# Attention heads with running sums in one bank: two key blocks give their values at once, and the scores share five banks

## The chip, the cores and the metric

The kernel runs on one core of a Trainium2 chip. Its engines are TensorE (PE, with its weight loads listed as PEld), VectorE (DVE), ScalarE (ACT), GpSimd (POOL) and SyncE (SP), whose queue issues all the DMAs. Each engine works through its own list of instructions in order and waits where a semaphore says so. Matmul results land in eight banks of PSUM, each 512 float32 columns wide on 128 partitions.

The metric is the time of one execution in microseconds of the device. Before the change it is 2222.45 us, the median of three runs (2220.9 to 2225.58).

## The reference

Four layers act on x of 2048 positions by 640 features, all in float32. Layers 1 and 3 are attention, layers 2 and 4 a Fourier mixing, and each is added to its input after a layer norm:

```
x = x + _A_ref(_layernorm(x), A_wqkv, A_wo)        # attention
x = x + _B_ref(_layernorm(x), seq_re, seq_im, hid_re, hid_im)
x = x + _A_ref(_layernorm(x), A_wqkv, A_wo)
x = x + _B_ref(_layernorm(x), seq_re, seq_im, hid_re, hid_im)
```

Attention has 32 heads of 20 features and a sliding window: position i sees positions j with 0 <= i - j < 256.

```
scores = einsum("bhqd,bhkd->bhqk", q, k) * (Dh ** -0.5)
mask = (idx[:, None] - idx[None, :] >= 0) & (idx[:, None] - idx[None, :] < W)
p = _softmax(where(mask, scores, -1e9))
o = einsum("bhqk,bhkd->bhqd", p, v);  out = o.reshape(B, S, D) @ wo
```

The Fourier layer multiplies by cosine and sine matrices over features and over positions and keeps the real part. The change leaves it alone.

## The kernel before, in words

Every layer takes its turn on the same core. The change lies in the part of an attention layer that the code calls heads (`heads`, line 597), which runs twice, once in each attention layer.

**Blocks and steps.** Positions are cut into 16 blocks of 128, heads into 8 groups of four ("quads"). With the window of 256, a key block meets at most three query blocks: its own and the next two. One step of the loop in line 770 is one key block of one quad, so there are 16 x 8 = 128 steps in an attention layer, after ten steps of lead. In each step the loop runs two halves, z = 0 and z = 1, for two of the four heads each. A half issues, in this order:

- T (`t_pair`, line 646; matmuls of line 650): the scores of key block t, with keys on the partitions, for its query blocks, up to 384 columns. Two heads run side by side in the upper and the lower 64 rows of the array, each into a bank of its own.
- S (`s_head`, line 617; matmuls of line 622): the scores of query block s = t + 10, this time with queries on the partitions, for two heads into two more banks. DVE adds the mask and takes the row maximum (line 627; the profile shows it as CUSTOM_DVE and DVE_READ_ACCUMULATOR2, which writes tile `mc`). The maximum is what T, ten steps later, gets subtracted through an extra row of its operands.
- the exponential (`t_exp`, line 654; ACT, line 660): both banks of T in one instruction, into tile `pt`; then POOL zeroes what lies outside the window (`t_mask`, lines 666 and 670).
- every fourth step, in z = 1: `m_rows` (line 632): PE transposes the maxima of four query blocks (line 635), ACT copies them negated (line 638) and SP sends them to the row of `qp`.
- in z = 1: PV (`pv`, line 676; matmuls of line 685): the products of exponentials and values for query block t - 1. For each of three key blocks and four heads it is one matmul of 128 columns with 32 columns of weights; the four heads stand side by side in the array. The twelve accumulate in one bank, and ACT copies its 128 columns to `ou` (line 692).
- in z = 0: `fill` (line 745): a few pairs of matmuls of other work. For most of the heads stage this is the projection of later quads (`project`, `pieces`, matmuls of line 253 in pairs of 64-row halves, 512 columns each), then the first three fifths of the output product (`partials`, 320 columns each).

Projection results leave their banks (6 and 7) by an ACT copy (line 540) and are cut into a high and a low part: POOL casts the high part (line 543), DVE subtracts (line 207). Jobs like these wait in lanes, one lane per engine, and `tick` (line 172) starts one of each lane at the end of every half.

**Banks.** T, S, PV and `m_rows` share six banks, 0 to 5. Which bank a use gets is settled when the program is written: `borrow` and `borrow_pair` (lines 136 and 144) keep for each bank the time at which it would be free by the constants of lines 40 to 42, and take the earliest. A T pair gets two neighbouring banks. The waits then follow from the tiles: an instruction that touches a bank waits for the last one that used it.

**Order.** All of this is written in one order by `heads`; no scheduler moves it. On each engine the instructions stand as the code issues them.

Of the kernel before, what the change touches and what calls it, by code (L numbers as in the profile page):

```python
# [40 lines left out]
AT_T, AT_S, AT_PV = (0.0, 1.28), (0.18, 1.46), 1.7  # L41
HELD_T, HELD_S, HELD_PV = 1.4, (0.96, 1.54), 1.3
# [5 lines left out]
    "m": (6, 7), "f": (6, 7, 4, 5), "w": (6, 7, 2, 3),  # L48
# [15 lines left out]
class Net:  # L64
# [71 lines left out]
    def borrow(self, at, *held):  # L136

        free = self.ring6
        got = sorted(free, key=lambda b: (free[b], b))[:len(held)]
        for b, d in zip(got, held):  # L140
            free[b] = max(at, free[b]) + d
        return got

    def borrow_pair(self, at, held):

        free = self.ring6
# [25 lines left out]
    def tick(self):  # L172
        self.slot += 1
        for k in sorted(k for k in self.posted if k <= self.slot):
            for f in self.posted.pop(k):
                f()
        for lane in self.lanes.values():
            if lane and lane[0][0] <= self.slot:
                lane.popleft()[2]()
# [18 lines left out]
    def sub_job(self, lane, key, lo, src, hi, done=None):  # L198

        eng = {"dve": self.nc.vector, "pool": self.nc.gpsimd}[lane]  # L200
        n = 2 if lane == "pool" else 1
        w = src.shape[-1] // n
        for i in range(n):
            c = slice(i * w, (i + 1) * w)

            def sub(c=c, last=i == n - 1):
                eng.tensor_tensor(out=lo[..., c], in0=src[..., c], in1=hi[..., c].bitcast(F32), op=OP.subtract)  # L207
                if last and done:
                    done()
            self.job(lane, key, sub)  # L210
# [141 lines left out]
    def attention(self, xsrc, xdst):  # L352
        self.take_small(F32)
        for name in ("kp", "qp"):
            for i in (1, 0):
                if (name, i) != ("kp", 0):
                    self.take_qk(name, i)
        self.after, self.wide, self.lead = False, False, True
        self.late_o, self.late_t, self.part_t, self.packable = [], 0, 0, set()
        self.before_heads(xsrc)  # L360
        self.heads(xsrc, xdst, self.fourier_hook)
        self.after_heads()
# [160 lines left out]
    def pieces(self, c, sbs, role):  # L523
# [13 lines left out]
        def copied(p, sb):  # L537
            st = self.work.tile([P, 2, 512], F32R, name="c", tag="c", bufs=3)
            r = self.raw()[:, :512]
            self.nc.scalar.activation(r, p, AF.Copy)  # L540

            def cast():
# [4 lines left out]
            def store():  # L547
                self.store_qk(c, sb, st)
                self.packable.add((c, sb))
            self.job("pool", ("qk", c, sb), cast)  # L550
# [46 lines left out]
    def heads(self, xsrc, xdst, hook):  # L597
# [56 lines left out]
        def t_exp(quad, kb, z, banks):  # L654
            n = min(NB - kb, 3)
            b0, b1 = banks
            if z == 0:
                i = 0 if (quad, kb) == (NQ - 1, NB - 1) else kb % 4
                pt[quad, kb] = self.pt[i].rearrange("p (h s) -> p h s", h=4)
            nc.scalar.activation(pt[quad, kb][:, 2 * z:2 * z + 2, :n * P], self.banks[:, b0:b1 + 1, :n * P],  # L660
                                 AF.Exp, scale=SCALE)
# [14 lines left out]
        def pv(quad, qb, bank):  # L676
# [4 lines left out]
            for kb in range(max(qb - 2, 0), qb + 1):  # L681
                t = pt[quad, kb]
                vq = self.vq[(4 * quad + kb // 4) % 3]
                for h in range(4):
                    nc.tensor.matmul(  # L685
                        self.banks[32 * h:32 * h + 32, bank, :P],
                        vq[:, 96 * (kb % 4) + 21 * h:96 * (kb % 4) + 21 * h + 32],
                        t[:, h, (qb - kb) * P:(qb - kb + 1) * P],
                        start=kb == max(qb - 2, 0), stop=kb == qb,
                        tile_position=(0, 32 * h), skip_group_check=True)  # L690
            pt.pop((quad, qb - 2), None)
            nc.scalar.activation(ous[quad, bk][:, at:at + P], self.banks[:, bank, :P], AF.Copy)
            if qb % 4 == 3:
                finish(quad, bk)
# [50 lines left out]
        def fill(n):  # L745

            k, size = 0, 1
            while k < size:
# [6 lines left out]
                if k == 1:  # L755
                    left = self.left + 1
                    size = -(-left // max(1, round(left / n)))
# [11 lines left out]
        self.ring6 = dict.fromkeys((0, 1, 2, 3), -99.0)  # L769
        for step in range(-LEAD, steps + 1):  # L770
            now[0] = step
            clock = step * STEP
            if step == -1:
                self.ring6.update({4: -99.0, 5: -99.0})
            if step + LEAD == steps + 1:
                for b in ROLES["w"]:
                    self.ring6.pop(b, None)
            self.wide, self.lead, self.tiled = step + LEAD > steps, step < -2, step < steps - 1
# [12 lines left out]
            if v >= 0 and v % 4 == 3:  # L791
                load_v(v // 4 + 2)
# [7 lines left out]
            rows = ((s - 1) // 16, ((s - 1) % 16) // 4) if 4 <= s < steps + 4 and s % 4 == 0 else None  # L800
            for z in range(2):
                if 0 <= t < steps:
                    banks = self.borrow_pair(clock + AT_T[z], HELD_T)
                    t_pair(t // 16, t % 16, z, banks)
                if 0 <= s < steps:
                    for e, b in enumerate(self.borrow(clock + AT_S[z], *HELD_S)):
                        s_head(s // 16, s % 16, 2 * z + e, b)
                if z and (rows or 0 <= v < steps):
                    last, = self.borrow(clock + AT_PV, HELD_PV)
                m = m_rows(*rows, last) if z and rows else iter(())  # L810
# [7 lines left out]
                if z:  # L818
                    if 0 <= v < steps:
                        pv(v // 16, v % 16, last)  # L820
                    for _ in m:
                        pass
                if z == 0 or t < -1 or t >= steps:
                    fill(nf)
# [121 lines left out]
    def partials(self, xsrc):  # L946
# [5 lines left out]
        for t in range(NB):  # L952
# [8 lines left out]
            ps = [self.bank("w" if self.wide else "m", 320) for _ in range(2)]  # L961
# [848 lines left out]
```

## Time and profile before

| | us |
|---|---|
| median of three runs | 2222.45 |
| the profiled execution, its own time | 2220.75 |
| its span, first instruction to last | 2219.0 |
| PE busy in the span | 2131.4 |
| DVE busy | 1669.5 |
| ACT busy | 1126.6 |
| POOL busy | 910.6 |
| first and last PV matmul of the program | 163.4 and 1638.6 |

The profile was taken on one execution; its times are microseconds from the start of the span unless marked ns. A busy PE includes the time that a result takes through the array, so a full row of it is no sign of a full array. The two heads stages lie at 163 to 538 us and at 1265 to 1639 us. PEclk is the granted clock of TensorE as a share of full speed. A releaser, named behind an arrow, is what ended a wait; a timeline row with a count covers several instructions of one kind that follow each other.

### The profile page before, as it was taken

The page shows a single profiled execution, that of the slowest core. Times are in us where ns is not written, and L with a number is a line of the kernel's source. Part 1 is how long each engine was busy: PE and PEld are TensorE (multiplying, and loading weights), DVE is VectorE, ACT ScalarE, POOL GpSimd, SP SyncE. Part 2 cuts the span into 40 slices and gives each one's busy share as a digit, 9 for nine tenths or more (in the row PEclk, how much of TensorE's full clock was granted, in tenths as well). Part 3 has the DMA queues.
Part 4 walks back from the last instruction along what each step waited for, and adds up shares of the span by engine and source line. Part 5 has one row for each costly group of instructions (what it writes and reads, how often), then busy time and mean ns, then how long its engine had stood idle before and what let it go on. Part 6 is the DMA issues. An engine that isn't in the chain of part 4 may idle for free.

```text
span 2219.0 us, 49084 instructions
## 1 busy us (share of the span) xinstructions
PE 2131.4 (96%) x17908; PEld 1786.0 (80%) x17908; DVE 1669.5 (75%) x4031; ACT 1126.6 (51%) x2101; POOL 910.6 (41%) x1456
## 2 busy tenths in 40 slices
PE   7999999998989999999999999998989999999999
PEld 7987777677868888889999777776777688888899
DVE  7368888785897968776651788887858978687776
ACT  3127776656554545552431377676655545455332
POOL 3016565666613223232330266566665132341334
PEclk9999999899999999999999999999999999999999
DMA  5545565775435354665646456657855354546653
GB/s 196 176 160 190 182 190 192 225 208 175 142 124 176 128 185 133 215 202 193 205 147 191 151 189 183 199 184 225 211 160 157 115 182 137 174 143 216 223 169 120
DMA packets 220177, 392.11 MB, mean 177 GB/s; under 512 B 39200, under 2 KB 85792, under 8 KB 219936
## 3 DMA queue, kind: packets, MB, share of 16 engines
q1 hardware_dynamic: 219936, 388.98, 55.6%
q8 instruction: 141, 2.31, 0.5%
q14 instruction: 100, 0.82, 0.1%
HBM read 273.94 MB, written 113.77 MB: 175 GB/s over the span
## 4 chain that ended last, share of the span: by engine, by line
PE 70%; DVE 13%; issue 6%; DMA 4%; ACT 3%; POOL 3%; SPq 0%; ACTq 0%; DVEq 0%; POOLq 0%
PE banks L1360 28%; PE banks L235 13%; PE banks L253 9%; PE banks L685 5%; PE banks L650 5%; DVE banks L627 5%; PE banks L1648 4%; PE banks L622 4%; DMA qp<-qk_d 1%; DVE c L207 1%; POOL big L228 1%; DVE mc L627 1%; DMA qk_d<-c 1%; DVE qp L228 1%; PE banks L337 1%
## 5 line engine op out<-in xcount | busy, mean ns | idle before, releaser
L627 DVE CUSTOM_DVE_ANT_0 banks<-banks,mask 128x384 f32<-128x384 f32 (+2 forms) x1024 | 526.8, 556 | 98.5 <-PE banks L622 80.5
L660 ACT ACTIVATE pt<-banks 128x768 f32<-128x768 f32 (+2 forms) x512 | 394.3, 772 | 179.0 <-PE banks L650 74.0
L666 POOL TENSOR_SCALAR_AFFINE_SELECT pt<-pt 128x256 f32<-128x256 f32 x512 | 215.8, 422 | 282.0 <-ACT pt L660 243.2
L253 PE MATMUL banks<-big,wc 64*128 64x512 f32 x1920 | 271.2, 394 | 0.4 <-DVE pt L438 0.4
L650 PE MATMUL banks<-qp,kp 61*128 61x384 f32 (+2 forms) x1024 | 211.8, 383 | 32.5 <-DVE mc L627 28.5
L685 PE MATMUL banks<-pt,vq 128*32 128x128 f32 x5760 | 213.4, 280 | 1.5 <-ACT pt L660 1.5
L622 PE MATMUL banks<-kp,qp 60*128 60x384 f32 (+2 forms) x1024 | 204.9, 352 | 6.6 <-DVE mc L627 4.1
L670 POOL TENSOR_SCALAR_AFFINE_SELECT pt<-pt 128x256 f32<-128x256 f32 x448 | 207.2, 462 | 0.0
L253 PEld LDWEIGHTS banks<-big,wc 64*128 64x128 f32 x1920 | 186.5, 185 | 22.9 <-ACT x L540 1.7
L650 PEld LDWEIGHTS banks<-qp,kp 61*128 61x128 f32 x1024 | 108.6, 186 | 100.4 <-DVE mc L627 76.5
L685 PEld LDWEIGHTS banks<-pt,vq 128*32 128x32 f32 x5760 | 143.4, 110 | 49.5 <-issue 36.4
L222 ACT ACTIVATE c<-pt 128x512 fp32r<-128x512 f32 x150 | 93.6, 626 | 160.3 <-POOL pt L1280 52.9
L222 ACT ACTIVATE qp<-pt 128x512 fp32r<-128x512 f32 (+1 forms) x195 | 119.9, 624 | 105.3 <-DVE pt L1294 54.0
L228 DVE TENSOR_TENSOR c<-pt,c 128x512 fp32r<-128x512 f32 x150 | 123.0, 822 | 52.0 <-ACT c L222 49.9
L228 DVE TENSOR_TENSOR qp<-pt,qp 128x512 fp32r<-128x512 f32 (+1 forms) x191 | 151.2, 799 | 11.7 <-ACT qp L222 9.0
L1360 PE MATMUL banks<-qp,big 128*128 128x512 f32 x630 | 152.4, 394 | 2.9 <-POOL qp L228 1.7
L1293 POOL TENSOR_TENSOR pt<-pt,pt 128x512 f32<-128x512 f32 x34 | 50.7, 1490 | 237.1 <-DMA pt<-c 145.9
L622 PEld LDWEIGHTS banks<-kp,qp 60*128 60x128 f32 x1024 | 119.9, 188 | 32.1 <-DVE mc L627 19.5
L627 DVE DVE_READ_ACCUMULATOR2_ANT mc<- 128x1 f32 x1024 | 144.3, 141 | 0.0
L1360 PEld LDWEIGHTS banks<-qp,big 128*128 128x128 f32 x630 | 119.0, 190 | 28.8 <-POOL qp L228 2.3
L1360 PE MATMUL banks<-qp,xc 128*128 128x512 f32 x480 | 117.2, 390 | 0.7 <-DVE xc L228 0.7
L543 POOL CAST c<-x 128x512 fp32r<-128x512 f32 x64 | 40.3, 633 | 181.3 <-ACT x L540 180.3
(246 smaller groups left out, 4475.0 us busy)
## 6 DMA issues: line engine op xcount, KB each, us to landing
pt<-c SPq DMA_DIRECT2D x188, 512.0 KB
qk_d<-c SPq DMA_DIRECT2D x80, 512.0 KB
kp<-qk_d SPq DMA_DIRECT2D x384, 80.0 KB
qp<-qk_d SPq DMA_DIRECT2D x384, 80.0 KB
kp<-u_d SPq DMA_DIRECT2D x32, 640.0 KB
o_d<-ou SPq DMA_DIRECT2D x64, 256.0 KB
x_d<-x SPq DMA_DIRECT2D x48, 320.0 KB
v_d<-pt SPq DMA_DIRECT2D x16, 768.0 KB
```

What stands on the lines that cost most here:

```text
L222: nc.scalar.activation(hi, src, AF.Copy, scale=-1.0 if neg else 1.0)
L228: (eng or nc.vector).tensor_tensor(out=lo, in0=src, in1=hi.bitcast(F32), op=OP.subtract)
L235: self.nc.tensor.matmul(p, x, y, start=n == 0, stop=n == last)
L253: self.nc.tensor.matmul(ps[a], x[r], y[r], start=half + i == 0, stop=half == 1 and i == n - 1, skip_group_check=True)
L622: nc.tensor.matmul(p, qp[quad % 2][b:b + 60, z, qb * P:(qb + 1) * P], kp[quad % 2][b:b + 60, z, k0 * P:(qb + 1) * P], start=True, stop=True)
L627: nc.vector.tensor_tensor_reduce(out=p, in0=p, in1=self.mask[:, 384 - n * P:], scale=1.0, scalar=NEG, op0=OP.add, op1=OP.max, accum_out=mc ...
L650: nc.tensor.matmul(self.banks[:, banks[e], :n * P], kp[quad % 2][b:b + 61, z, kb * P:(kb + 1) * P], qp[quad % 2][b:b + 61, z, kb * P:(kb + ...
L660: nc.scalar.activation(pt[quad, kb][:, 2 * z:2 * z + 2, :n * P], self.banks[:, b0:b1 + 1, :n * P], AF.Exp, scale=SCALE)
L666: nc.gpsimd.affine_select(out=t[:, :, 0:P], in_=t[:, :, 0:P], pattern=[[0, 2], [1, P]], compare_op=OP.is_ge, fill=0.0, base=0, channel_mul ...
L670: nc.gpsimd.affine_select(out=t[:, :, 256:384], in_=t[:, :, 256:384], pattern=[[0, 2], [-1, P]], compare_op=OP.is_gt, fill=0.0, base=0, ch ...
L685: nc.tensor.matmul(self.banks[32 * h:32 * h + 32, bank, :P], vq[:, 96 * (kb % 4) + 21 * h:96 * (kb % 4) + 21 * h + 32], t[:, h, (qb - kb) ...
L1360: nc.tensor.matmul(self.banks[:, bk, :], p, b[q], start=start and m == 0, stop=stop and last and m == 2, skip_group_check=True)
```

## The change

Six things change, all in the heads stage:

1. PV runs every second step, for two key blocks at once, and is turned around: each key block gives its values to all its query blocks (up to 384 columns in one matmul of each head, or two where the columns wrap). The sums run on in bank 5, which holds four query blocks of 128 columns. No matmul starts a sum; instead ACT writes zeros over a pair of query blocks (`clear`) after it has copied them out (`sums`, 256 columns instead of two copies of 128). `v` is t - 2.
2. T, S and `m_rows` share five banks, 0 to 4. A T pair takes the two banks that are free first, whether they are neighbours or not, and its exponential reads them as one slice with a step. New constants say when and how long a bank is held, and S and `m_rows` of a half may not take the banks of its T pair.
3. `fill` gets exact sizes: nine pairs in z = 0 and none in z = 1 of a step with PV, five and four in the step without; while projections last, about three quarters of the rate and none, then a half and a half.
4. The low part of the projection results is subtracted by POOL in two pieces of 256 columns instead of by DVE in one of 512, in a chain that starts only while fewer than three `c` buffers are in use.
5. In the lead, `tick` starts two jobs of each lane.
6. The banks 2 and 3 are no longer used for the last outputs within the heads stage.

```diff
-AT_T, AT_S, AT_PV = (0.0, 1.28), (0.18, 1.46), 1.7
-HELD_T, HELD_S, HELD_PV = 1.4, (0.96, 1.54), 1.3
+AT_T, AT_S, AT_M = ((0.0, 0.95), (0.4, 1.45)), 0.18, 1.5
+HELD_T, HELD_S, HELD_M = 1.4, (0.96, 1.54), 1.2
+SUMS = 5
+SIZES = ((9, 0), (5, 4))
...
     def borrow_pair(self, at, held):
-        free = self.ring6
-        b = min((b for b in free if b + 1 in free),
-                key=lambda b: (max(free[b], free[b + 1], at), -min(free[b], free[b + 1]), b))
-        free[b] = free[b + 1] = max(free[b], free[b + 1], at) + held
-        return b, b + 1
+        free = self.ring5
+        got = sorted(sorted(free, key=lambda b: (free[b], b))[:2])
+        for b in got:
+            free[b] = max([at] + [free[b] for b in got]) + held
+        return got
...
-            st = self.work.tile([P, 2, 512], F32R, name="c", tag="c", bufs=3)
             r = self.raw()[:, :512]
+            key = "qk", c, sb
             self.nc.scalar.activation(r, p, AF.Copy)
...
+            def lead():
+                if self.c_live == 3:
+                    self.post(1, lambda: self.job("pool", key, lead))
+                    return
+                self.c_live += 1
+                st = self.work.tile([P, 2, 512], F32R, name="c", tag="c", bufs=3)
                 self.nc.gpsimd.tensor_copy(st[:, 0, :], r)
-                self.sub_job("dve", ("qk", c, sb), st[:, 1, :], r, st[:, 0, :],
-                             lambda: self.post(2, store))
+                self.sub_job("pool", key, st[:, 1, :], r, st[:, 0, :], lambda: self.post(2, lambda: store(st)))
...
-            nc.scalar.activation(pt[quad, kb][:, 2 * z:2 * z + 2, :n * P], self.banks[:, b0:b1 + 1, :n * P],
+            nc.scalar.activation(pt[quad, kb][:, 2 * z:2 * z + 2, :n * P], self.banks[:, b0:b1 + 1:b1 - b0, :n * P],
                                  AF.Exp, scale=SCALE)
...
+        def pv(quad, kb):
+            n, a = min(NB - kb, 3), kb % 4
+            vq = self.vq[(4 * quad + kb // 4) % 3]
+            t = pt.pop((quad, kb))
+            d0 = 0
+            while d0 < n:
+                d1 = min(n, d0 + 4 - (a + d0) % 4)
+                at = (a + d0) % 4 * P
+                for h in range(4):
+                    nc.tensor.matmul(
+                        self.banks[32 * h:32 * h + 32, SUMS, at:at + (d1 - d0) * P],
+                        vq[:, 96 * (kb % 4) + 21 * h:96 * (kb % 4) + 21 * h + 32],
+                        t[:, h, d0 * P:d1 * P], start=False, stop=d0 == 0,
+                        tile_position=(0, 32 * h), skip_group_check=True)
+                d0 = d1
+        def clear(c0, c1):
+            nc.scalar.activation(self.banks[:, SUMS, c0:c1], self.half.broadcast_to([P, c1 - c0]), AF.Copy, scale=0.0)
...
-            nc.scalar.activation(ous[quad, bk][:, at:at + P], self.banks[:, bank, :P], AF.Copy)
-            if qb % 4 == 3:
+            nc.scalar.activation(ous[quad, bk][:, at:at + 2 * P], self.banks[:, SUMS, at:at + 2 * P], AF.Copy)
+            clear(at, at + 2 * P)
+            if at:
                 finish(quad, bk)
...
-            s, t, v = step + LEAD, step, step - 1
+            s, t, v = step + LEAD, step, step - 2
...
-                if z == 0 or t < -1 or t >= steps:
-                    fill(nf)
+                if not 0 <= t < steps:
+                    if z == 0 or t < -1 or t >= steps:
+                        fill(nf)
+                elif not (z and visit):
+                    fill(SIZES[not visit][z] if done[0] >= total else round(nf * (0.75 if visit else 0.5)), True)
```

What it moves shows in the built programs. In the rows below, names stand as in the code (`pt`, `ou`, `banks`), the sizes are those of the output, and the brackets hold the semaphores that an instruction waits for, each named after the engine that raises it. `half` as a source marks `clear`.

ACT in steps 57 to 59 of layer 1 (quad 3), before: the copy of PV (L692) stands behind every second exponential (L660), and the copy of the maxima (L638) behind it in every fourth step.

```order
L660 ACTIVATE pt_95<-banks 128x768 [waits PE_49,Activation_49,Pool_49]
L660 ACTIVATE pt_95<-banks 128x768 [waits PE_49,Pool_49]
L692 ACTIVATE ou_98<-banks 128x128 [waits DMAHW3_49,DMAHW2_49,PE_49]
L660 ACTIVATE pt_96<-banks 128x768 [waits PE_49,Activation_49,Pool_49]
L660 ACTIVATE pt_96<-banks 128x768 [waits PE_49,Pool_49]
L692 ACTIVATE ou_98<-banks 128x128 [waits PE_49]
L638 ACTIVATE mt<-banks 16x128 [waits DMAHW1_49,DMAHW0_49,Activation_49]
```

ACT at the same place after, steps 56 to 58; the exponentials are L668, the copies L709, the zeros L702.

```order
L668 ACTIVATE pt_94<-banks 128x768 [waits DVE_49,Pool_49] x2
L709 ACTIVATE ou_99<-banks 128x256 [waits PE_49,Activation_49]
L702 ACTIVATE banks<-half 128x256 [waits Activation_49]
L668 ACTIVATE pt_95<-banks 128x768 [waits PE_49,Pool_49]
L668 ACTIVATE pt_95<-banks 128x768 [waits DVE_49,Pool_49]
L668 ACTIVATE pt_96<-banks 128x768 [waits DVE_49,Pool_49]
L668 ACTIVATE pt_96<-banks 128x768 [waits DVE_49,PE_49,Pool_49]
L709 ACTIVATE ou_98<-banks 128x256 [waits DMAHW0_49,DMAHW1_49,PE_49,Activation_49]
```

In the rows before, an exponential waits for PE, that is for its own two T matmuls, and for things long done. In the rows after, five of the six wait for DVE. Where a T pair lies in banks 0 and k, the slice with a step is treated as all the banks from 0 to k, and a maximum of S that works in a bank between them counts as a writer. The semaphore's count says which: it is the maximum of an S head of the same half, issued just ahead of the exponential. So it is in 163 of the 236 halves of layer 1 that have an S: in 132 it is the second head's, in 31 the first's; the other 73 have their pair in banks 0 and 1, or no S between.

PE around a PV with `m_rows`, steps 74 and 75 of layer 1, before. L622 is S, L635 the transposition of the maxima, L685 PV, L650 T.

```order
L622 MATMUL banks<-kp_103,qp_104 128x384 [waits DVE_49]
L622 MATMUL banks<-kp_103,qp_104 128x384 [waits Activation_49]
L635 MATMUL banks<-ident,mc 16x128
L685 MATMUL banks<-pt_97,vq_93 32x128 x4
L685 MATMUL banks<-pt_94,vq_91 32x128 x4
L685 MATMUL banks<-pt_95,vq_91 32x128 [waits Pool_49]
L685 MATMUL banks<-pt_95,vq_91 32x128
L685 MATMUL banks<-pt_95,vq_91 32x128 [waits Pool_49]
L685 MATMUL banks<-pt_95,vq_91 32x128
L650 MATMUL banks<-qp_105,kp_560 128x384 [waits DVE_49]
L650 MATMUL banks<-qp_105,kp_560 128x384
L622 MATMUL banks<-kp_103,qp_104 128x384 [waits Activation_49]
```

PE around such a PV after, steps 58 and 59; the two S matmuls of the half (L630) stand just ahead of these rows. L643 is the transposition, L694 PV, L658 T.

```order
L643 MATMUL banks<-ident,mc 16x128 [waits DVE_49]
L694 MATMUL banks<-pt_94,vq_93 32x384 [waits DMAHW4_49,Pool_49]
L694 MATMUL banks<-pt_94,vq_93 32x384
L694 MATMUL banks<-pt_94,vq_93 32x384 [waits Pool_49]
L694 MATMUL banks<-pt_94,vq_93 32x384
L694 MATMUL banks<-pt_95,vq_93 32x384 [waits Pool_49]
L694 MATMUL banks<-pt_95,vq_93 32x384
L694 MATMUL banks<-pt_95,vq_93 32x384 [waits Pool_49]
L694 MATMUL banks<-pt_95,vq_93 32x384
L658 MATMUL banks<-qp_104,kp_103 128x384 [waits Activation_49]
L658 MATMUL banks<-qp_104,kp_103 128x384
L630 MATMUL banks<-kp_560,qp_105 128x384 [waits Activation_49]
```

Twelve PV matmuls of 128 columns in each step became eight of 384 in every second one (sixteen where columns wrap). The transposition now takes the bank of an S head of its own half and waits for its maximum; S of the next half takes that bank and waits for ACT's copy of the transposed rows. The first T head has bank 0 in 234 of those 236 halves, so it waits for the exponential of the half before.

More of the change, by code (lines that the diff above doesn't have):

```diff
@@ L817, in heads @@
                     self.relieve()
[L818 to L822, printed above, removed]
[L823 to L824 removed]
+                if z and visit:
+                    for kb in (v % 16, v % 16 + 1):
+                        pv(v // 16, kb)
+                    sums(v // 16, v % 16)
+                for _ in m:
+                    pass
+                if not 0 <= t < steps:
[3 more added lines that the diff above has]
+                    fill(SIZES[not visit][z] if done[0] >= total else round(nf * (0.75 if visit else 0.5)), True)
                 self.tick()
```

70 lines of the change are left out of this document (30 added, 40 removed).

## The prediction

> **What bounds the kernel now.** I read the page first, for what the heads stage does most.
>
> ```profile
> span 2219.0 us, 49084 instructions
> ...
> L627 DVE CUSTOM_DVE_ANT_0 banks<-banks,mask 128x384 f32<-128x384 f32 (+2 forms) x1024 | 526.8, 556 | 98.5 <-PE banks L622 80.5
> L660 ACT ACTIVATE pt<-banks 128x768 f32<-128x768 f32 (+2 forms) x512 | 394.3, 772 | 179.0 <-PE banks L650 74.0
> ```
>
> The span is 1.75 us under the execution's own 2220.75, which lies 1.7 under the median; my sum goes from 2220.75. The maxima cost DVE more than the exponentials cost ACT, and neither waits much. Next the busy times by windows, of the exponentials alone, and of all engines for the middle of the stage. A step holds two exponentials, so half the count is steps.
>
> ```profile
> 163.00:438.00 275.00, 148.05 (x192) 0.97 0.62 194
> 163.00:515.00 352.00, 183.96 (x239) 0.98 0.65 196
> 515.00:538.00 23.00, 10.76 (x16) 1.00 0.32 97
> 208.00:386.00 178.00, 98.60 (x128) 1.00 0.60 189
> 208.00:386.00 178.00, 171.73 (x2442) 130.14 (x2437) 153.42 (x559) 126.47 (x232) 107.16 (x255) 1.00 0.60 189
> ```
>
> While projections last, 96 steps take 275 us, 2.86 each. The next 23.5 steps (47 exponentials in 77 us), with the output product, take 3.28 each; the last 8, without S, 2.9. In the middle PE is busy for 172 of 178 us and DVE for 153: all engines overlap, PE and DVE bind together. The timeline of one step shows how:
>
> ```profile
> 1380.03 0.45 PE L650 MATMUL banks<-qp,kp 61*128 61x384 f32 x2
> 1380.16 0.28 ACT L692 ACTIVATE ou<-banks 128x128 f32<-128x128 f32 x1 [0.33 <-PE banks L685]
> 1380.31 0.34 PE L622 MATMUL banks<-kp,qp 60*128 60x384 f32 x2
> 1380.49 0.86 PE L253 MATMUL banks<-big,wc 64*128 64x512 f32 x6
> 1380.59 0.81 ACT L660 ACTIVATE pt<-banks 128x768 f32<-128x768 f32 x1
> 1380.68 0.57 DVE L627 CUSTOM_DVE_ANT_0 banks<-banks,mask 128x384 f32<-128x384 f32 x1 [0.53 <-PE banks L622]
> 1381.16 0.14 DVE L627 DVE_READ_ACCUMULATOR2_ANT mc<- 128x1 f32 x1
> 1381.16 0.60 DVE L627 CUSTOM_DVE_ANT_0 banks<-banks,mask 128x384 f32<-128x384 f32 x1
> 1381.39 0.60 ACT L540 ACTIVATE x<-banks 128x512 f32<-128x512 f32 x1
> 1381.68 0.14 DVE L627 DVE_READ_ACCUMULATOR2_ANT mc<- 128x1 f32 x1
> 1381.83 0.86 PE L685 MATMUL banks<-pt,vq 128*32 128x128 f32 x24
> 1382.62 0.45 PE L650 MATMUL banks<-qp,kp 61*128 61x384 f32 x2
> 1382.84 0.87 DVE L207 TENSOR_TENSOR c<-x,c 128x512 fp32r<-128x512 f32 x1
> ```
>
> From T to T of the next step pass 2.59 us. The exponential starts while the two maxima of its half have yet to run: the two branches after T and S are parallel. That is what the change touches.
>
> **The change part by part.** *The exponential's wait.* After the change, five exponentials in seven wait for a maximum of their own half, and the next half's T waits for that exponential (its bank 0). So T, S, maximum, exponential and next T stand in one chain, and nothing of a later half can begin beside it on PE. Two more links of that chain, from the timeline near the end of the stage (T, exponential, T) and from one place where an exponential now follows a maximum:
>
> ```profile
> 517.90 0.81 ACT L660 ACTIVATE pt<-banks 128x768 f32<-128x768 f32 x1 [0.69 <-PE banks L650]
> ...
> 518.76 0.44 PE L650 MATMUL banks<-qp,kp 61*128 61x384 f32 x2 [0.17 <-ACT pt L660]
> ...
> 519.31 0.81 ACT L660 ACTIVATE pt<-banks 128x768 f32<-128x768 f32 x1 [0.37 <-PE banks L650]
> ```
>
> ```profile
> 361.60 0.14 DVE L627 DVE_READ_ACCUMULATOR2_ANT mc<- 128x1 f32 x1
> 361.79 0.81 ACT L660 ACTIVATE pt<-banks 128x768 f32<-128x768 f32 x1 [0.41 <-DVE mc L627]
> ```
>
> A half whose exponential waits for the second head's maximum ("S1") lasts: T to S 0.28 (1380.03 to 1380.31), S to maximum 0.37, both maxima 1.14 (1380.68 to 1381.82), to the exponential 0.05 (361.74 to 361.79), itself 0.81, to the next T 0.05 (518.71 to 518.76): 2.70 us. With the first maximum alone (0.62, to 1381.30) it is 2.18 ("S0"). Where only T is waited for ("P") it is 0.55 (518.76 to 519.31) + 0.81 + 0.05 = 1.41.
>
> *PV, the transposition, the copies.* Two rows of PE where the transposition of the maxima goes ahead of PV:
>
> ```profile
> 401.54 0.28 PE L635 MATMUL banks<-ident,mc 128*16 128x128 f32 x1
> 401.75 0.86 PE L685 MATMUL banks<-pt,vq 128*32 128x128 f32 x24
> ```
>
> Two steps had two PVs of 24 rows of 128 columns (a float32 matmul shows as two rows), 1.72 in all. After, they have one of 16 rows of 384 columns, the same columns in a third of the rows. By columns it costs the 1.72 less one of the two ends, a result's way through the array (a pair of T shows 0.45 from start to end for 384 columns, a set of PV rows some 0.27): 1.45. By rows it would be 0.57, 16 of 24 rows at 0.86. I take columns, since pairs of other widths differ with the width (three of 512 columns took 0.86, one of 384 took 0.34), and keep 0.57 as the low end. In an S1 half, PV (0.28 + 0.29 + 1.45 = 2.02) hides behind the chain's 2.70. Every second visit the transposition must wait for the first maximum (0.28 + 0.37 + 0.62 + 0.05 = 1.32), with PV behind it (0.21 + 1.45), and T behind PV: 3.0. The next half's S then waits for ACT's copy of the transposed rows, which stands behind the copy of the sums and the zeros; S starts some 0.7 late: 2.9 instead of 2.18. Copies: two of 0.28 become one of 256 columns and one clear, 0.38 each by interpolation between 0.28 (128 columns) and 0.60 (512); they lie on ACT in a gap of the chain (0.81 busy in 2.70) except there.
>
> *The sum at full clock.* In 12 steps the 24 halves, by the semaphores: z = 0 with PV to follow, 4 S1 and 2 P, 13.6; z = 1 with PV, 3 S1 and 3 with transposition, 17.1; z = 0 after it, one S0, two at 2.9, three P of 1.7 (PV's tail still in the way), 13.2; z = 1 without PV, 13.6. Together 57.5, 4.79 a step. Steps with short T and S take off 0.2, and fill's wait for a bank's second copy (every 8 steps) adds 0.15: 4.74 against 2.86.
>
> *The clock.* Windows across the two places where PE had least to do in this stage; the third figure from the right is the granted clock.
>
> ```profile
> 417.00:420.00 3.00, 2.04 (x32) 1.16 (x32) 3.00 (x9) 1.85 (x5) 3.00 (x6) 1.00 0.56 171
> 420.00:424.00 4.00, 3.71 (x36) 2.36 (x38) 2.69 (x11) 1.81 (x4) 1.74 (x5) 0.57 0.89 252
> 424.00:427.00 3.00, 2.50 (x31) 1.42 (x29) 2.28 (x8) 1.13 (x2) 1.51 (x3) 0.50 0.93 275
> ...
> 434.00:437.00 3.00, 3.00 (x32) 2.60 (x26) 1.99 (x9) 1.09 (x2) 1.21 (x4) 0.50 0.65 176
> ...
> 1519.00:1523.00 4.00, 2.66 (x37) 1.53 (x37) 3.91 (x14) 2.46 (x5) 2.91 (x7) 1.00 0.67 186
> ```
>
> PE busy for 2.04 of 3 us brought the clock to half; it came back only after a stretch with PE full (3.00 of 3). 2.66 of 4 kept it. After the change a chain half without PV has T 0.45, S 0.34 and one or two pairs of fill (0.86/3 = 0.29 each), about 1.1 to 1.3 of 2.70, under half: the clock must fall there. What a half lasts then, from the second half of those rows' stretch (PE, and DVE's next maximum):
>
> ```profile
> 430.96 0.69 PE L650 MATMUL banks<-qp,kp 61*128 61x384 f32 x2
> 431.45 0.52 PE L622 MATMUL banks<-kp,qp 60*128 60x384 f32 x2
> 432.01 0.57 DVE L627 CUSTOM_DVE_ANT_0 banks<-banks,mask 128x384 f32<-128x384 f32 x1 [1.24 <-PE banks L622]
> 433.31 1.51 PE L685 MATMUL banks<-pt,vq 128*32 128x128 f32 x24
> ```
>
> T to S 0.49, S to maximum 0.56: S1 3.10, S0 2.58, P 1.65 to 2.1. PV, twice 1.51 less a tail, about 2.7, no longer hides: 3.7 with PV, 4.85 with the transposition too. The 12 steps take 72.5, and with the same edges 6.0 each. A PV half then fills PE, and may bring the clock back if such a stretch falls right, for a stretch: I take four fifths at half clock, 4.74 + 0.8 x 1.26 = 5.75. With PV at its low end it would be 5.3.
>
> [...]
>
> *What moves off the chain.* DVE loses the subtractions (0.87 each, one in two steps), POOL gets two of 256 columns for each; the nearest row of POOL:
>
> ```profile
> L885 POOL TENSOR_TENSOR x<-x,rr x48: 724/734/1047, 405.7 to 1613.6; 128x256 f32<-128x256 f32 x48
> ```
>
> 1.47 us in two steps of POOL, which is busy 107 of 178 and would have steps twice as long: hidden, at nothing; DVE's gain is worth nothing either, since the maxima wait for S now. Without the chain it would be up to 0.4 a step, which the last rival uses. The bigger tick in the lead, the later `c` buffer and the last outputs' banks lie in spare time. Where projections end, the steps before wait for loads (the exponentials again):
>
> ```profile
> 415.00:438.00 23.00, 8.32 (x13) 0.63 0.77 232
> ```
>
> 6.5 steps at 3.54 instead of the 2.78 of the stage's middle: 5 us, which longer steps absorb, -5 a layer.
>
> *The sum.* A layer: 96 x (5.75 - 2.86) = 277; the later 23.5 steps have more fill (nine, five and four pairs), so the clock holds better: 4.6 at full and 6.0 at half clock, 4.9 taken, 23.5 x (4.9 - 3.28) = 38; the last eight, without S, 3.2 for 2.9, 3; loads -5. That is 313, twice 626: 2220.75 + 626 = 2847 us.
>
> **The rivals.** *Full clock throughout.* PV and fill in visits keep the clock up, as 1519 to 1523 did with 2.66 of 4: 96 x 1.88 = 180, 23.5 x 1.32 = 31, 3, -5: 209 a layer, 2639 us. *All at half clock*: 301 + 63 + 12 - 5 = 371, 2963.
>
> *The exponential isn't held by the maxima* (DVE's mark is reached early, because S ran ahead): then only T, exponential, T binds. Four steps have six halves of 1.41, one with PV at 2.0, one with the transposition at 3.0, and 0.5 trails behind these: 14.0, 3.5 a step. That is 61, and 7 for the later steps, 68 a layer, 2357. Against it: T, S and the exponential's wait belong to one half, and S stands behind T in PE's list.
>
> *Faster.* The waits cost nothing, because ring and order give way, and PV is paid by instruction (0.57 for 1.72 in two steps). DVE then bounds a step, freed of its subtraction: its four maxima take 2.28, the quiet step above 2.59, and between them 2.45 instead of 2.86 gives 96 x 0.41 x 2 = 79, 2142 us. It decides if an S1 half takes under 1.4 us, which two maxima of 1.14 in front of an exponential of 0.81 exclude. It would need the semaphore not to hold at all.
>
> That the change does nothing has no room: the wait and the bank 0 are in the program.
>
> **How the numbers follow.** The serial chain at mostly half clock 0.60 (2847; some 2760 with PV at its low end); the same at full clock 0.20; all half or worse, say through late loads, 0.10; 2357 0.06; faster 0.03; no change 0.01. The range leaves out the last three and most of the "worse": 2620 to 2960. What a measurement here can tell from no change is some 0.2%, 4.4 us; by the cases, faster 0.03, same 0.01, slower 0.96.
>
> **What would show it.** In the profile after: ACT idle ahead of L668 on `mc`, released by DVE, in some 160 of 236 halves a layer; PE idle ahead of L658 on `pt`, released by ACT; 5 to 6 us for two exponentials in the middle of the stage; PEclk near 0.5 to 0.6 in the heads slices; PV rows about three times longer in streaming, visits under 3 us at full clock; L643 waiting for DVE. Wrong would be the forecast if the clock stays at 1.00 (then 2639), if exponentials start before their half's maxima end (2357 or less), or if steps exceed 6.5 us, which loads or POOL's masks and subtractions on the chain would do.

## The result, and the profile after

The changed kernel takes 2877.2 us (median of 4 runs, 2866.9 to 2884.5) against 2223.2 us, a ratio of 1.294 (95% interval 1.289 to 1.299). The profiled execution took 2882.5 us, 1.7 more than its span; so its sums stand 5 us above the median.

The page, first the lines that answer to those shown of before:

```profile
span 2880.8 us, 43356 instructions
...
L635 DVE CUSTOM_DVE_ANT_0 banks<-banks,mask 128x384 f32<-128x384 f32 (+2 forms) x1024 | 528.0, 557 | 779.2 <-PE banks L630 765.3
L668 ACT ACTIVATE pt<-banks 128x768 f32<-128x768 f32 (+2 forms) x512 | 393.2, 769 | 715.8 <-DVE mc L635 577.3
```

The same instructions take the same time, 557 ns a maximum and 769 an exponential. What grew is the idle time ahead of them: 779 us before the maxima, which wait for S (98.5 before), and 716 before the exponentials (179.0), 577 of it ended by DVE's maxima. How much of the waiting before the exponentials DVE's maxima ended, in both layers, before and then after (us, times):

```profile
  DVE mc L627: 4.5, 11
```

```profile
  DVE mc L635: 577.3, 290
```

Windows of the exponentials alone: the 96 steps with projections, the next 24, the last 8, and then the same 178 us that were shown of before. The fifth row has all engines in these 178 us; in the window rows PEclk stands third from the right.

```profile
163.00:723.00 560.00, 147.92 (x193) 0.68 0.32 97
723.00:841.00 118.00, 37.30 (x48) 0.92 0.50 136
841.00:864.00 23.00, 11.13 (x16) 1.00 0.27 80
208.00:386.00 178.00, 45.79 (x61) 0.66 0.30 91
208.00:386.00 178.00, 129.26 (x807) 70.92 (x807) 69.78 (x256) 63.37 (x110) 57.85 (x134) 0.66 0.30 91
```

Two exponentials are a step: 5.80 us a step for 2.86, 4.9 for 3.28, 2.9 for 2.9. No engine is full any more: PE 129 of 178 us (172 before), DVE 70 (153), at two thirds of the clock. This is the picture of a chain. One half of it at full clock, on the timeline:

```profile
407.57 0.45 PE L658 MATMUL banks<-qp,kp 61*128 61x384 f32 x2 [0.35 <-ACT pt L668]
...
407.86 0.37 PE L630 MATMUL banks<-kp,qp 60*128 60x384 f32 x2
...
408.23 0.57 DVE L635 CUSTOM_DVE_ANT_0 banks<-banks,mask 128x384 f32<-128x384 f32 x1 [0.18 <-PE banks L630]
...
408.71 0.60 DVE L635 CUSTOM_DVE_ANT_0 banks<-banks,mask 128x384 f32<-128x384 f32 x1
409.23 0.14 DVE L635 DVE_READ_ACCUMULATOR2_ANT mc<- 128x1 f32 x1
409.47 0.81 ACT L668 ACTIVATE pt<-banks 128x768 f32<-128x768 f32 x1 [1.94 <-DVE mc L635]
...
410.33 0.69 PE L658 MATMUL banks<-qp,kp 61*128 61x384 f32 x2 [1.42 <-ACT pt L668]
```

T to S 0.29, S to maximum 0.37, the maxima 1.14 to 409.37, 0.10, the exponential 0.81, 0.05: from T to T 2.76 us, in which PE waits for 1.42. The next half, from 410.33 on, has the transposition and PV, now at half clock:

```profile
412.05 0.38 PE L643 MATMUL banks<-ident,mc 128*16 128x128 f32 x1 [0.72 <-DVE mc L635]
412.36 2.79 PE L694 MATMUL banks<-pt,vq 128*32 128x384 f32 x16
415.08 0.69 PE L658 MATMUL banks<-qp,kp 61*128 61x384 f32 x2
416.31 0.69 PE L630 MATMUL banks<-kp,qp 60*128 60x384 f32 x2 [0.54 <-ACT mt L646]
```

From T at 410.33 to T at 415.08 it takes 4.75 us: the transposition waits for the maximum, PV follows, and the next S waits for ACT's copy. The windows around it show the clock go:

```profile
406.00:410.00 4.00, 2.42 (x18) 1.55 (x18) 2.28 (x8) 1.43 (x3) 1.54 (x4) 1.00 0.43 131
410.00:413.00 3.00, 1.95 (x9) 0.79 (x13) 1.14 (x4) 0.65 (x2) 0.77 (x2) 0.56 0.00 0
413.00:416.00 3.00, 2.77 (x18) 0.68 (x10) 0.00 (x0) 1.14 (x3) 0.77 (x2) 0.50 0.03 5
```

PE was busy for 2.42 of 4 us, and the clock went to half. The trace lists every change of the clock. In this stage of this run the granted clock was either full or half (1.00 or 0.50), and its changes lay 3.41 us or whole multiples of that apart. Here are four stretches of this length, in each of which the clock was constant: after the first it rose to full, through the second it stayed there, after the third it fell to half, after the fourth it rose.

```profile
400.11:403.52 3.41, 3.17 (x36) 1.89 (x36) 1.25 (x5) 0.99 (x2) 0.79 (x3) 0.50 0.50 163
403.52:406.93 3.41, 2.15 (x24) 1.30 (x16) 1.16 (x5) 1.80 (x4) 1.51 (x4) 1.00 0.26 82
406.93:410.35 3.42, 1.65 (x16) 0.92 (x12) 2.26 (x8) 1.40 (x2) 0.77 (x3) 1.00 0.27 74
427.42:430.83 3.41, 3.41 (x36) 2.02 (x28) 0.69 (x6) 2.23 (x4) 1.47 (x3) 0.50 0.00 0
```

Over the first heads stage, 168 to 864 us, the clock fell after 37 such stretches, in which PE was busy for 19 to 60%, and stayed full through 53 with 55 to 100%. It rose after 38 with 84 to 100%, and stayed at half through 74 with 29 to 93%. Between 55 and 60% both are found, a fall and none, and from 84 to 93% both a rise and none, so PE's busy share alone doesn't tell the cases apart. The waits of PE in the heads stage of layer 1, summed (us, times, longest):

```profile
PE banks L658 <- ACT pt L668: 133.3, 139, 2.1
PE banks L643 <- DVE mc L635: 20.7, 29, 1.2
PE banks L630 <- ACT mt L646: 20.3, 29, 0.9
PE banks L256 <- ACT x L543: 17.0, 12, 2.2
```

No single wait is longer than 2.2 us, and still a third of the clock is missing in the steps with projections.

### The profile page after: what moved, and what is told of

Its sections match the earlier page's. It is cut to its first block, busy times and chain, and to the rows that moved or that the text cites. A ratio compares the mean times of both kernels' runs of the same rounds, so it can differ in the third digit from the quotient of the medians.

```text
span 2880.8 us, 43356 instructions
## 1 busy us (share of the span) xinstructions
PE 2441.5 (85%) x14964; PEld 1835.4 (64%) x14964; DVE 1636.9 (57%) x3967; ACT 1160.6 (40%) x2103; POOL 981.4 (34%) x1584
## 4 chain that ended last, share of the span: by engine, by line
PE 62%; ACT 12%; DVE 11%; issue 7%; DMA 4%; POOL 3%; SPq 1%; ACTq 0%; DVEq 0%; POOLq 0%
PE banks L1382 22%; PE banks L238 10%; PE banks L694 8%; ACT pt L668 7%; PE banks L256 7%; PE banks L658 6%; DVE banks L635 5%; PE banks L630 4%; PE banks L1670 4%; DVE mc L635 2%; ACT ou L709 1%; PE banks L643 1%; POOL big L231 1%; ACT mt L646 1%; PE banks L340 1%
## 5 line engine op out<-in xcount | busy, mean ns | idle before, releaser
L635 DVE CUSTOM_DVE_ANT_0 banks<-banks,mask 128x384 f32<-128x384 f32 (+2 forms) x1024 | 528.0, 557 | 779.2 <-PE banks L630 765.3
L668 ACT ACTIVATE pt<-banks 128x768 f32<-128x768 f32 (+2 forms) x512 | 393.2, 769 | 715.8 <-DVE mc L635 577.3
L658 PE MATMUL banks<-qp,kp 61*128 61x384 f32 (+2 forms) x1024 | 283.1, 512 | 270.8 <-ACT pt L668 267.8
L674 POOL TENSOR_SCALAR_AFFINE_SELECT pt<-pt 128x256 f32<-128x256 f32 x512 | 213.2, 416 | 875.3 <-ACT pt L668 858.5
L658 PEld LDWEIGHTS banks<-qp,kp 61*128 61x128 f32 x1024 | 137.3, 234 | 515.9 <-ACT pt L668 449.1
L256 PE MATMUL banks<-big,wc 64*128 64x512 f32 x1920 | 379.3, 489 | 34.6 <-ACT x L543 33.8
L256 PEld LDWEIGHTS banks<-big,wc 64*128 64x128 f32 x1920 | 235.7, 239 | 69.8 <-ACT x L543 50.1
L630 PE MATMUL banks<-kp,qp 60*128 60x384 f32 (+2 forms) x1024 | 241.8, 428 | 42.1 <-ACT mt L646 40.8
L694 PE MATMUL banks<-pt,vq 128*32 128x384 f32 (+2 forms) x2816 | 276.8, 545 | 0.0
L630 PEld LDWEIGHTS banks<-kp,qp 60*128 60x128 f32 x1024 | 147.4, 247 | 68.8 <-ACT mt L646 57.6
L678 POOL TENSOR_SCALAR_AFFINE_SELECT pt<-pt 128x256 f32<-128x256 f32 x448 | 186.1, 415 | 0.0
L694 PEld LDWEIGHTS banks<-pt,vq 128*32 128x32 f32 x2816 | 98.4, 142 | 105.5 <-issue 82.7
L635 DVE DVE_READ_ACCUMULATOR2_ANT mc<- 128x1 f32 x1024 | 145.3, 142 | 0.0
L709 ACT ACTIVATE ou<-banks 128x256 f32<-128x256 f32 x128 | 49.0, 383 | 135.3 <-PE banks L694 135.2
```

The lines of the kernel that those rows point to most:

```text
L256: self.nc.tensor.matmul(ps[a], x[r], y[r], start=half + i == 0, stop=half == 1 and i == n - 1, skip_group_check=True)
L630: nc.tensor.matmul(p, qp[quad % 2][b:b + 60, z, qb * P:(qb + 1) * P], kp[quad % 2][b:b + 60, z, k0 * P:(qb + 1) * P], start=True, stop=True)
L635: nc.vector.tensor_tensor_reduce(out=p, in0=p, in1=self.mask[:, 384 - n * P:], scale=1.0, scalar=NEG, op0=OP.add, op1=OP.max, accum_out=mc ...
L658: nc.tensor.matmul(self.banks[:, banks[e], :n * P], kp[quad % 2][b:b + 61, z, kb * P:(kb + 1) * P], qp[quad % 2][b:b + 61, z, kb * P:(kb + ...
L674: nc.gpsimd.affine_select(out=t[:, :, 0:P], in_=t[:, :, 0:P], pattern=[[0, 2], [1, P]], compare_op=OP.is_ge, fill=0.0, base=0, channel_mul ...
L678: nc.gpsimd.affine_select(out=t[:, :, 256:384], in_=t[:, :, 256:384], pattern=[[0, 2], [-1, P]], compare_op=OP.is_gt, fill=0.0, base=0, ch ...
```

## The experiments

**Two ways to take the maxima out of the chain.** First, neighbouring banks again:

```
-        got = sorted(sorted(free, key=lambda b: (free[b], b))[:2])
-        for b in got:
-            free[b] = max([at] + [free[b] for b in got]) + held
-        return got
+        b = min((b for b in free if b + 1 in free),
+                key=lambda b: (max(free[b], free[b + 1], at), -min(free[b], free[b + 1]), b))
+        free[b] = free[b + 1] = max(free[b], free[b + 1], at) + held
+        return b, b + 1
```

> The changed kernel, with one thing put back: a T pair takes two neighbouring banks again (of five), so that its exponential's slice holds no third bank. In the built program no exponential waits for a maximum of its own half. Theory (the wait for the maxima puts T, S, maximum and exponential in one chain, and PE's idle time in it halves the clock): the chain is T, exponential, T in about half of the halves, 3.0 to 3.7 us a step, the clock near 1.00 through the heads, 2300 to 2420 us. Rival (the turned PV, its zeros and copies, and the exact fill are what costs): 2700 us or more, with steps of 5 us.

2386.3 us, ratio to before 1.072 (1.069 to 1.074). Second, the change's own banks, but one exponential for each bank:

```
-            nc.scalar.activation(pt[quad, kb][:, 2 * z:2 * z + 2, :n * P], self.banks[:, b0:b1 + 1:b1 - b0, :n * P],
-                                 AF.Exp, scale=SCALE)
+            for e in range(2):
+                nc.scalar.activation(pt[quad, kb][:, 2 * z + e, :n * P], self.banks[:, banks[e], :n * P],
+                                     AF.Exp, scale=SCALE)
```

> The changed kernel with the exponential of a half as two instructions, one for each bank of the T pair; the banks stay as the change picks them, and T's first head still takes bank 0. No exponential waits for a maximum. Theory: as with neighbouring banks the maxima leave the chain; two exponentials of 384 columns cost about 0.49 each (from 0.60 at 512 and 0.81 at 768), but the next T waits for the first of them alone: 2280 to 2400 us, clock near 1.00. Rival (bank 0 held from half to half is the cause, not the maxima): 2600 us or more. Rival (PV and fill): 2700 or more.

2389.9 us, ratio 1.075 (1.072 to 1.077). The exponentials by windows, with neighbouring banks and then with two exponentials for each half:

```profile
208.00:386.00 178.00, 74.05 (x98) 0.97 0.48 143
```

```profile
208.00:386.00 178.00, 82.52 (x200) 0.99 0.50 149
```

49 and 50 steps in 178 us, 3.6 each, where the change does 30.5; the clock is back (0.97 and 0.99 for 0.66). Both edits take the wait for the maxima out, each in another way, and both bring some 490 us. Neither changes the wait alone: the first also takes T off bank 0 in about two thirds of the halves, worked through the code, the second frees bank 0 after the first of two exponentials. What they share is the wait, and the second still reads the two distant banks. So the slice with a step costs by what it is taken to touch, and not by reading distant banks; the exponential itself took no longer (769 ns for 772). All the rest of the change, the turned PV and bank 0 among it, makes 161 to 164 us net without the wait.

**The clock alone.** The chain stays, and PE is given matmuls that change nothing, in 79 of the 256 halves of a layer (counted from the rows of T, 2604 for 1024):

```
                     for e, b in enumerate(self.borrow(at + AT_S, *HELD_S, but=banks)):
                         s_head(s // 16, s % 16, 2 * z + e, b)
+                    if banks and banks[0] < b < banks[1] and not (z and visit):
+                        for _ in range(5):
+                            t_pair(t // 16, t % 16, z, banks)
```

> The changed kernel, and in every half whose exponential waits for the second head's maximum and which has no PV, the two T matmuls are issued five times more behind S. They write what already stands there, and 0.8 us of matmuls fit into the 1.5 us in which PE waits there, so they prolong no chain. Theory (a third of the loss is the clock, which falls because PE idles): the granted clock in the heads rises from 0.67 to over 0.9, steps go from 5.8 to about 4.9 us, 2640 to 2740 us. Rival (the low clock is no cause: what it slows is hidden in the chain, or it doesn't follow PE's idle time): 2860 us or more.

2765.0 us, ratio 1.242 (1.240 to 1.244). The 96 steps with projections, exponentials alone, then the steps after them:

```profile
160.00:654.00 494.00, 147.67 (x192) 0.92 0.36 109
654.00:782.00 128.00, 37.91 (x49) 0.87 0.48 127
```

More work on PE made the kernel 112 us faster. The clock went from 0.68 to 0.92, the steps from 5.80 to 5.15. That is less than I expected, and the later steps, with more fill of their own, got longer (5.2 for 4.9, their clock 0.87 for 0.92), so the added matmuls were not all free. At least 112 of the 654 us are the clock.

**The banks' choice alone, in the kernel before.** Six banks, the old PV; only `borrow_pair` (not printed again) and the slice of the exponential are the change's:

```
...
-            nc.scalar.activation(pt[quad, kb][:, 2 * z:2 * z + 2, :n * P], self.banks[:, b0:b1 + 1, :n * P],
+            nc.scalar.activation(pt[quad, kb][:, 2 * z:2 * z + 2, :n * P], self.banks[:, b0:b1 + 1:b1 - b0, :n * P],
```

> The kernel before with the banks of a T pair picked as the change picks them, the two that are free first, and the slice with a step; six banks, PV and all else as before. 82 exponentials of 512 then wait for the second maximum of their half, 134 for the first. Theory: such halves take 2.70 and 2.18 us instead of 1.43 where the next T waits for the exponential, which 226 T matmuls now do: some 100 us a layer if all of it shows, about half if the third pair of banks gives slack: 2300 to 2500 us. Rival (ACT has time to wait, the wait alone costs nothing and five banks are needed for the loss): 2215 to 2240 us.

2637.9 us, ratio 1.184 (1.181 to 1.188), more than I expected at the most. The waits in the first heads stage, to 515 us, and the exponentials there:

```profile
ACT pt L660 <- DVE mc L627: 81.6, 60, 3.3
...
PE banks L685 <- ACT pt L660: 65.4, 46, 2.3
```

```profile
163.00:515.00 352.00, 121.84 (x159) 0.88 0.39 122
```

79.5 steps in the time of 119.5, at 4.4 us. I had counted only the exponentials that wait for maxima. Here PV, too, waits for late exponentials (46 times, 65 us), and the clock fell to 0.88. Worked through `borrow` with the constants of this kernel, PV's bank lies between the two banks of its own half's T pair in 80 of the 128 steps of a layer, and in none of the kernel before. So the slice makes a second false wait: PV stands behind an exponential that reads a bank on either side of PV's own, but never that one. The trace shows the wait; the bank follows from the code. This one edit, without any other part of the change, makes 412 us.

**POOL's subtraction alone, in the kernel before.** The new chain of copy, cast and two subtractions of 256 columns, of which these lines are a part:

```
...
-                self.sub_job("dve", ("qk", c, sb), st[:, 1, :], r, st[:, 0, :],
-                             lambda: self.post(2, store))
+                self.sub_job("pool", key, st[:, 1, :], r, st[:, 0, :], lambda: self.post(2, lambda: store(st)))
```

> The kernel before with the change's fourth part alone: POOL subtracts the low part of the projection results in two pieces of 256 columns, in the chain that starts while fewer than three buffers are in use. DVE loses 64 subtractions of 0.84 us, 27 us a layer of a stage where it is busy 153 of 178 us. If DVE binds as much as PE there: 2190 to 2215 us. If PE alone sets the pace, or POOL's longer chain delays its masks: 2218 to 2235 us.

2215.4 us, ratio 0.9956 (0.9943 to 0.9968): 9 us below the kernel before, small but clear of the interval. In the middle of the stage (all engines):

```profile
208.00:386.00 178.00, 175.47 (x2506) 133.68 (x2500) 147.74 (x557) 128.95 (x237) 125.30 (x292) 1.00 0.61 192
```

DVE is less busy (148 for 153), PE more (175 for 172). Of 54 us that DVE is spared in two layers, 9 arrive: the time lies 0.4 us above the first case. PE, busy for 175 of the 178 us, is the likely next bound; I didn't test that.

**The transposition.** From the kernel with two exponentials: the transposition takes the fifth bank, and ACT copies it ahead of the sums.

```
+                    taken = self.borrow(at + AT_S, *HELD_S, but=banks)
...
+                    banks = tuple(banks) + tuple(taken)
...
                 m = m_rows(*rows, *self.borrow(clock + AT_M, HELD_M, but=banks)) if z and rows else iter(())
...
+                for _ in m:
+                    pass
                 if self.heavy:
...
                     sums(v // 16, v % 16)
-                for _ in m:
-                    pass
```

> The kernel with two exponentials for each half, and the transposition of the maxima takes the fifth bank instead of one of its own half's S, and ACT copies it right behind the exponential instead of behind the sums and the zeros. The halves with transposition and PV took 2.88 us at full clock there, those with PV alone 1.85. Theory (the transposition waits for a maximum of its own half, PV and the next T stand behind it): 58 such halves fall to about 1.9 us, and the halves after them lose their wait for the copied rows: 2310 to 2345 us. Rival (PV's length binds there anyway): 2375 us or more.

2301.6 us, ratio 1.035 (1.033 to 1.037). The waits of PE in the kernel with two exponentials, 165 to 460 us:

```profile
PE banks L630 <- ACT mt L646: 16.3, 20, 0.9
PE banks L643 <- DVE mc L635: 10.6, 20, 0.6
```

Neither of these rows is left in the list after the edit. From T to T, in the same stretch at full clock, the halves with both transposition and PV fell from 2.83 to 2.24 us on average, and the halves right behind them from 1.96 to 1.40. With 58 of each in the two layers that is 34 and 32 us of the 88 gained. The time came out 8 us below my range, since I had priced the first kind alone and said of the second only that it would lose its wait. The two parts of the edit were not run apart.

**PV in every step.** From the kernel with the moved transposition: one key block each, all fill in z = 0 and the constants `AT_T` for the time of T as before the change; first with two exponentials, then with one and neighbouring banks:

```
-                if z and visit:
-                    for kb in (v % 16, v % 16 + 1):
-                        pv(v // 16, kb)
-                    sums(v // 16, v % 16)
+                if z and 0 <= t - 1 < steps:
+                    pv((t - 1) // 16, (t - 1) % 16)
+                    if t % 2 == 0:
+                        sums(v // 16, v % 16)
...
```

> As the kernel with the moved transposition, and PV runs in every step for one key block (the sums' copy and zeros stay in every second), with the fill of before, all of it in z = 0. Theory (two key blocks at once make a half of 1.85 us that the other three, at 1.4 to 1.6, don't give back, since five banks let no work run ahead): halves of about 1.45, steps of 2.9 to 3.1, 2240 to 2300 us. Rival (the rest of the loss lies in five banks, not in the lump of PV): no gain over the kernel with the moved transposition, 2320 us or more.

> The same as the kernel with PV in every step, but with one exponential for each half and the T pair in neighbouring banks. T then waits for exponentials in more cases (312 matmuls, and for their full 0.81 us): 2250 to 2320 us, some 10 us above the split one. Rival (two exponentials of 384 columns load ACT more than the earlier release of bank 0 is worth): 10 to 30 us below it.

2226.8 us, ratio 1.0008 (0.9997 to 1.0019), and 2249.8 us, ratio 1.010 (1.009 to 1.012). The first, in the middle of the stage, and its PV of one key block:

```profile
208.00:386.00 178.00, 175.06 (x1676) 109.90 (x1672) 140.58 (x532) 137.36 (x351) 122.28 (x285) 1.00 0.58 183
```

```profile
302.66 0.85 PE L695 MATMUL banks<-pt,vq 128*32 128x384 f32 x8
```

PE is as full as in the kernel before. Eight rows of 384 columns take 0.85 us, 24 rows of 128 took 0.86: PV is paid by columns here, and a third of the instructions saves nothing. The first came out below my range and the second at its edge: the lump of two key blocks, with the fill and the constants that go with it, cost 75 us. Two exponentials with the banks that are free first are 23 us better than one with neighbouring banks; that this is the earlier release of a bank is argued, not shown apart from the choice of banks.

In steps, then: 2877 for the change, 2390 without the false wait, 2302 with the transposition moved, 2227 with PV spread. What is left of the change there, the running sums, five banks, the clears and the POOL subtraction, now with two exponentials, comes out even with the kernel before, but 11 us above that kernel with the POOL subtraction alone.

## Why the prediction was right, point by point

The forecast was 2847 us with 2620 to 2960; measured were 2877, 1% more, by the way that was named.

- *The exponential's wait*: right. ACT idles ahead of L668 for DVE's maxima, 290 of the 512 times in both layers together by the profile, against "some 160" of 236 that the semaphores give for each; where the maximum is early enough no idle time would show. The half at 407.57 took 2.76 for 2.70. Taking the wait out by two different edits gave back 490 us.
- *PV, the transposition, the copies*: right in size. 4.75 us at half clock for 4.85. At full clock PV of two key blocks took 1.50 in the kernel with repeated matmuls (the row at 400.24 us of its timeline), for 1.45, so the low end of 0.57 is excluded. The wait of S for ACT's copy was there (0.54 in the row at 416.31).
- *The sum at full clock and the clock's share*: two errors that cancel, so that 1% is luck. I took a step of 4.74 us at full clock and four fifths of the time at half. The granted clock of 0.68 means 0.64 of the time at half. A line through the change (5.80 at 0.64) and the kernel with repeated matmuls (5.15 at a clock of 0.92, so 0.16) gives some 4.9 at full and 6.3 at half clock, where I had 4.74 and 6.0; as that kernel's added matmuls were not wholly free, 4.9 is an upper estimate. So the chain was mis-sized by some 4%, and the share of half clock by 16 points. The missing 0.2 us lie in the halves without PV. By the starts of T from 163 to 723 us, those that ran at full clock nearly throughout took 2.36 us on average for my 2.24, and those at half clock 2.81 for 2.60. The halves with PV were no longer than I said: 2.78 for 2.85 at full clock (six of them), and at half clock 4.57 with the transposition and 3.65 without, for 4.85 and 3.7. One of my sums is also off: z = 0 after PV adds up to 13.1, not 13.2, which is 0.01 a step.
- *The clock*: the sign and the cause were right; PE filled again brought the clock back with the chain left in place. I had seen it come back only after a stretch with PE full; in the changed kernel the least busy stretch before a rise had 84% of its 3.41 us. That may be why the share of half clock came out lower. No wait of PE was longer than 2.2 us there, and still the clock fell. The longest pause within a stretch was 0.8 to 2.1 us where it fell and up to 1.6 where it stayed full; PE's busy share was 19 to 60% where it fell and 55 to 100% where it stayed.
- *The later steps*: 4.9 forecast, 4.9 measured, at a clock of 0.92. *The last eight*: 2.9 for the 3.2 forecast.
- *What moves off the chain*: nothing in the changed kernel's profile speaks against "hidden", with POOL busy for 58 of 178 us; it wasn't run apart there. I misread how often the subtraction comes: the trace of before has 24 of them in the 96 steps with projections, one in four steps and not one in two, so it is 0.2 us a step and not 0.4. That DVE's relief is worth something where no chain stands showed in the kernel before (-9 us), a sixth of what DVE was spared. The faster rival's 2142, built on 0.4 a step, overrated it.
- *The rivals at full clock throughout* (2639) and *all at half clock* (2963) are excluded by the clock, 0.68 in the projecting steps, and the one *in which the exponential isn't held* (2357) by the 290 waits; but this last one describes the kernels without the wait: 2386 and 2390, 30 us above its figure.

## What to carry to other kernels

Before two distant pieces are read as one slice with a step, look which instructions between them the program then takes for writers: the number and the engine of the semaphores on the instruction tell it ahead of any run. The wait that closed a loop over PE, DVE and ACT cost twice here, as a chain and by the clock that came with PE's pauses: 2877 us with it, 2386 and 2390 by the two edits without it, and at least 112 us of the loss came by the clock alone (0.68 in the projecting steps, 0.92 with more matmuls on PE). So ask of such a wait both what it delays and how much it leaves PE to do. When PV or a like block of work is gathered into fewer and wider matmuls, price it by columns first, as it came out here (0.85 us for 8 rows of 384 columns, 0.86 for 24 of 128), and ask who waits while the lump runs.

## What the runs showed of the hardware that wasn't expected

Five more pairs of matmuls in 79 of the 256 halves of a layer, with no use at all, shortened the program by 112 us (2877 to 2765), the granted clock going from 0.68 to 0.92 in the projecting steps. The choice of banks alone, read as one slice, turned a kernel of 2225 us into one of 2638: PV's waits for late exponentials there, 46 times and at most 2.3 us long, came with a loss of a tenth of the clock (0.88 for 0.98). And in the changed kernel's first heads stage (168 to 864 us) the clock fell to half 37 times, each after 3.41 us with PE busy for 19 to 60% of them, though no pause of PE was longer than 2.3 us.
